# The first FFN product of batches 2 to 8 by Strassen's method, with the second weights streamed from HBM

## The chip, the cores and the metric

One core of a Trainium2 chip runs the program. The metric is device time in microseconds, median of three runs. Engines are called as in the profile: PE (TensorE matmul), PEld (its weight load), DVE (VectorE), ACT (ScalarE), POOL (GpSimd), SP (SyncE, which issues the DMAs here).

## What is computed

A local and global attention over 8 batches, 8 heads, 512 local and 32 global positions, head size 64, then a feed-forward network over all 8 x (512 + 32) tokens:

```python
x = attn_out.transpose(0, 2, 1, 3).reshape(B * S, H * D)     # 4352 x 512
h = x @ w_in                                                 # w_in: 512 x 2048
g = np.maximum(h, 0.0) + alpha * np.minimum(h, 0.0)
return (g @ w_out).astype(np.float32)                        # w_out: 2048 x 512
```

A local query sees the 32 global keys and the keys at most 32 positions away; a global query sees all keys. The weights arrive as float64.

## The kernel before

**Two streams in one loop.** The feed-forward work is cut into nine groups G: the eight batches' local tokens (512 columns each) and, last, all 256 global tokens. A group has 16 units, one per 128 of the 2048 hidden features (f). Unit t = 16 G + f does the first product `f1(t)` and, two units late (`LAG`), the second product `f2(t - 2)`. Attention goes on beside it: a head pair P (two heads of a batch, so four pairs per batch) is done in four steps u = 4 P + s, one per unit, with u = t + 19 (`NPRE`), so that a batch's attention is ready before its group begins. `attn(u, where)` is called at three places of a unit: "pre" before `f1`, "mid" after it, "post" between the two parts of `f2`. Head pairs 0 to 3 and most of pair 4 are done ahead of unit 0 in `prelude()`.

**Products in three terms.** Weights and activations are float32 and are split into a high part (a cast to float32r) and a low part (the rest); a product is high x high + low x high + high x low, three matmuls. `f1` contracts 512 = 4 x 128 channels, so 12 matmuls of 512 columns into one bank `h`, of which there are two. DVE turns `h` into `g` in two operations (L350, L351), ACT casts `gh` (L353), POOL forms `gl` (L354). `f2` part 0 multiplies `gh` by the two weight parts (8 matmuls), part 1 multiplies `gl` by the high part (4 matmuls), into four banks `o0` to `o3` that collect over the group's 16 units.

**Weights.** 32 pieces (f, j), j = 0 for w_in and 1 for w_out, are loaded as float64, decoded (`decode_words`, ACT, DVE and POOL) and split (`split_weights`) during the prelude and the first 12 or so units, and then stay in 32 of the 33 tiles of the pool `w`.

**Attention of a head pair.** Step 0: scores (`local_scores`, 64 small matmuls into two banks `s`) and softmax of both heads (DVE adds the mask and takes the minimum, ACT does eight exps); step 1: the sums' reciprocals and POOL's multiplication (`tail`); step 2: `values(P)`, which multiplies the values of the pair before (`pv_all`, into banks `s`), scores the global queries of this pair and writes `x_raw` (`pv_out`, ACT L319, L320), and then the global softmax. The probabilities must be transposed: for P below 8 (`NRAW`) by PE (`transpose_pe`, into banks `s`, copied to `pt`), later by DVE's 32x32 transposes (L287) and a round trip through HBM (`transpose_q`, `fetch_pt`). `split_x` splits `x_raw` into `xh` and `xl`, four channel blocks per group, in the last unit of the group before.

**What sets the order.** Matmuls stay in program order. For the other engines and SP a planner with a simulated time line picks, among the instructions that are ready, the one of highest priority; priority is program order, and attention's instructions are put ahead by 50. An engine executes its queue strictly in the order picked. All matmuls are recorded under the helper's line L88, so the tile names tell them apart: `h_ps`, `o`, `s_ps`, `o_ps`, `g_ps`, `pt`.

Of the kernel before, what the change touches and what calls it, by code (L numbers as in the profile page):

```python
# [8 lines left out]
F32 = mybir.dt.float32  # L9
F32R = mybir.dt.float32r  # L10
# [4 lines left out]
ALU = mybir.AluOpType  # L15
AX = mybir.AxisListType

NB, NH, SL, SG, D = 8, 8, 512, 32, 64
NPAIR = 4
DM, DF = 512, 2048  # L20
NF = DF // 128
NC = DM // 128
# [3 lines left out]
NEG = -8.0e9  # L26
WARM = (16, 12, 8, 8, 8)
NRAW = 8
NWB = 33
NST = 18  # L30
CLAMP_LO = 2.0**-15
CLAMP_HI = 122880.0 - 2.0**-7
TC = dict(schedule_with_timeline_sim=True)
HP = 50
NPRE = 19
HP0 = 400
LAG = 2
GOFF = 1024
GROWS = {1: (0, 0), 4: (0, 1), 7: (0, 2), 10: (1, 0), 13: (1, 1), 15: (1, 2)}
PRE = 3  # L40
RATE = (2, 1)
GROUPS = [("l", b) for b in range(NB)] + [("g", 0)]


# [12 lines left out]
def longformer_ffn(ctx: ExitStack, tc: tile.TileContext, qk, v, w, alpha, out):  # L57
    nc = tc.nc
# [3 lines left out]
    work = ctx.enter_context(tc.tile_pool(name="work", bufs=1))  # L62
    psum = ctx.enter_context(tc.tile_pool(name="psum", bufs=1, space=PS))

    dram = ctx.enter_context(tc.tile_pool(name="dram", bufs=1, space=bass.MemoryType.DRAM))
# [21 lines left out]
    def matmul(*a, **k):  # L87
        ins = nc.tensor.matmul(*a, **k)  # L88
        tc.keep_in_program_order(ins)
        return ins  # L90

    def stage(name, dtype=F32):
        return work.tile([128, 512], dtype, tag="st", name=name, bufs=NST)

    wraw, wts = {}, {}

    ordered = [True]

# [24 lines left out]

    def split_weights(f, j):
        t = wmid.pop((f, j))
        wt = wpool.tile([128, 2, 512], F32R, tag="w", name="wt")
        nc.scalar.copy(wt[:, 0, :], t)  # L127
        nc.gpsimd.tensor_tensor(wt[:, 1, :], t, wt[:, 0, :].bitcast(F32), op=ALU.subtract)  # L128
        wts[f, j] = wt

    consts = stage("consts")
    ident = consts[:, 384:512]
# [37 lines left out]
    def local_scores(P, warm=0):  # L170
        t = qks[P]
        sbanks[P] = [bank("h" if P < NPAIR and P % 2 else "s", "s_ps") for h in range(2)]
        keep_warm(sbanks[P][0], warm)
        masked = P < NRAW
        if masked:
            for h in range(2):
                matmul(sbanks[P][h], identb, bits, start=True, stop=False, skip_group_check=True)
        for i in range(4):
            for c in range(4):
                b = 4 * i + c  # L180
                k0 = NQ + 32 * start(b)
                for h in range(2):
                    th = t[64 * h : 64 * h + 64]
                    matmul(sbanks[P][h][32 * c : 32 * c + 32, 128 * i : 128 * i + 128], th[:, 32 * b : 32 * b + 32], th[:, k0 : k0 + 128], start=not masked, stop=True, skip_group_check=masked)
        ps[P] = work.tile([128, 1024], F32, tag="p", name="p", bufs=2)

    def p_tile(P, h, i):
        if P < NRAW:
# [78 lines left out]

    def new_pt(P):
        if P not in pts:
            pts[P] = work.tile([128, 1408], F32, tag="pt", name="pt", bufs=2)  # L270
        return pts[P]

    def transpose_pe(P, x, warm=0):
        pb = bank(f"o{x}" if P < NPAIR else "s", "pt")
        keep_warm(pb, warm)
        src, n = (ps[P][:, 512 * x : 512 * x + 512], 4) if x < 2 else (sg_sb, 3)
        for i in range(n):
            tc.keep_in_program_order(nc.tensor.transpose(pb[:, 128 * i : 128 * i + 128], src[:, 128 * i : 128 * i + 128], ident))  # L278
        copy("ada"[x], new_pt(P)[:, 512 * x : 512 * x + 128 * n], pb[:, 0 : 128 * n])
# [47 lines left out]
    def split_x(G, c):  # L327
        kind, b = GROUPS[G]
        n = SL if kind == "l" else NB * SG
        src = (x_raw if kind == "l" else x_glb)[:, c, 0:n]  # L330
        xh, xl = stage("xh", F32R), stage("xl", F32R)
        nc.scalar.copy(xh[:, 0:n], src)
        nc.vector.tensor_tensor(xl[:, 0:n], src, xh[:, 0:n].bitcast(F32), op=ALU.subtract)  # L333
        xs[G, c] = (xh, xl)

    gs, obs, gpart = {}, {}, {}

    def f1(T):
        G, f = divmod(T, NF)
        n = SL if GROUPS[G][0] == "l" else NB * SG  # L340
        h = bank("h", "h_ps")
        k = 0
        for c in range(NC):
            cs = slice(128 * c, 128 * c + 128)
            xh, xl = xs[G, c]
            for j, xt in ((0, xh), (1, xh), (0, xl)):
                matmul(h[:, 0:n], wts[f, 0][:, j, cs], xt[:, 0:n], start=(k == 0), stop=(k == 11))
                k += 1
        g = stage("g")
        nc.vector.tensor_scalar(g[:, 0:n], h[:, 0:n], 0.0, alpha_sb[:, f : f + 1], op0=ALU.min, op1=ALU.mult)  # L350
        nc.vector.scalar_tensor_tensor(g[:, 0:n], h[:, 0:n], 0.0, g[:, 0:n], op0=ALU.max, op1=ALU.add)  # L351
        gh, gl = stage("gh", F32R), stage("gl", F32R)
        nc.scalar.copy(gh[:, 0:n], g[:, 0:n])  # L353
        nc.gpsimd.tensor_tensor(gl[:, 0:n], g[:, 0:n], gh[:, 0:n].bitcast(F32), op=ALU.subtract)  # L354
        gs[T] = (gh, gl)

    def f2(T, part):
        G, f = divmod(T, NF)
        kind, b = GROUPS[G]
        n = SL if kind == "l" else NB * SG  # L360
        if f == 0 and part == 0:
            obs[G] = [psum.tile([128, 512], F32, tag=f"o{m}", name=f"o{m}", bufs=1) for m in range(NC)]
        o = obs[G]
        gh, gl = gs[T]
        for m in range(NC):
            ms = slice(128 * m, 128 * m + 128)
            if part == 0:
                matmul(o[m][:, 0:n], wts[f, 1][:, 0, ms], gh[:, 0:n], start=(f == 0), stop=False)
                matmul(o[m][:, 0:n], wts[f, 1][:, 1, ms], gh[:, 0:n], start=False, stop=False)
            else:  # L370
                matmul(o[m][:, 0:n], wts[f, 1][:, 0, ms], gl[:, 0:n], start=False, stop=(f == NF - 1))
        if part == 0:
            return
        del gs[T]
        if f == NF - 1:
            col = b * SL if kind == "l" else NB * SL
            for m in range(NC):
                st = stage("ost")
                copy("ad"[m % 2] if kind == "g" else "a", st[:, 0:n], o[m][:, 0:n])
                nc.sync.dma_start(out[m, :, col : col + n], st[:, 0:n])  # L380
# [52 lines left out]
    def attn(u, where):  # L433
        P, s = divmod(u, 4)
        if u == NPRE:
            if where == "mid":
                transpose_pe(P, 0)
                transpose_pe(P, 1)
            if where == "post":
                transpose_pe(P, 2)  # L440
                load_qk(P + 2)
            return
        if not (live(P) or live(P - 1)):
            return
        if (s, where) == (0, "pre") and live(P):
            local_scores(P)
        if s < 2 and where == "pre" and live(P):
            tails.append(softmax(P, s))
        if where == "mid":
            while tails:  # L450
                tails.pop()()
        if live(P) and P < NRAW:
            if (s, where) == (2, "pre"):
                transpose_pe(P, 0)
                transpose_pe(P, 1)
            if (s, where) == (3, "mid"):
                transpose_pe(P, 2)
        if (s, where) == (2, "mid"):
            gpart[P] = global_bank(P)
            values(P, "s")  # L460
            if live(P):
                load_v(P)
        if not live(P):
            return
        if (s, where) == (2, "post"):
            global_softmax(P)
            if live(P + 2):
                load_qk(P + 2)
        if P >= NRAW:
            if (s, where) == (2, "pre"):  # L470
                transpose_q(P, 0)
            if (s, where) == (3, "pre"):
                fetch_pt(P, 0)
                transpose_q(P, 1)
            if (s, where) == (3, "post"):
                fetch_pt(P, 1)
        if P == NRAW - 1 and (s, where) == (3, "post"):
            nc.gpsimd.memset(sg_sb[:, 288:384], 0.0)
# [35 lines left out]
    prelude()  # L514
    ordered[0] = False
    NT = len(GROUPS) * NF
    for t in range(NT + LAG):
        u = t + NPRE
        with tc.high_priority(offset=HP):
            attn(u, "pre")  # L520
        G, f = divmod(t + 1, NF)
        last = t + 1 < NT and f == 0
        if t < NT:
            f1(t)
        if last:
            for c in range(NC - 1):
                split_x(G, c)
        with tc.high_priority(offset=HP):
            attn(u, "mid")
        if last:  # L530
            split_x(G, NC - 1)
        if t >= LAG:
            f2(t - LAG, 0)
        with tc.high_priority(offset=HP):
            attn(u, "post")
        if t >= LAG:
            f2(t - LAG, 1)
        weights_step(RATE[t % 2])


_OUT = (NC, 128, NB * (SL + SG))
# [51 lines left out]
```

## Time and profile before

| | us |
|---|---|
| runs | 994.74, 995.45, 997.18 |
| median | 995.45 |
| profiled execution | 996.93, of which the span is 994.9 |
| PE busy | 940.0 of the span |
| DVE, ACT, POOL busy | 468.0, 350.3, 332.5 |
| unit 0 begins | 83.5 |
| global group | about 940 to the end |

The page gives busy time per engine, and groups of instructions as "line engine operation, output<-inputs, shape, count | busy, mean ns | idle before, releaser". The stage view gives the same busy times per stretch of the span, with the granted PE clock (1.00 is full), the share of time in which the DMA engines are busy, and GB/s. The chain is the sequence of work that ended last, as "start, us, what xcount"; the timeline has "start, us, engine line operation ... xcount [idle before <-releaser]". A busy PE overlaps its matmuls, so a matmul's own row is longer than its distance to the next one.

### The profile page before, as it was taken

How to read it: one execution, taken by the hardware profiler on the slowest of the kernel's cores; microseconds unless marked ns; L12 is line 12 of the kernel's file. 1: busy time of each engine (PE TensorE's matmuls, PEld its weight loads, DVE VectorE, ACT ScalarE, POOL GpSimd, SP SyncE). 2: the span in 40 equal slices, each digit the busy share in tenths (PEclk: the TensorE clock that was granted, in tenths of full speed). 3: DMA queues.
4: the chain of work that ended last, by engine and by line, in shares of the span. 5: the costliest groups of instructions: out<-in, count | busy, mean ns of one | idle time of the engine just before them, and what ended most of it. 6: DMA issues, size and time to landing. Idle time of an engine off the chain costs nothing.

```text
span 994.9 us, 19937 instructions
## 1 busy us (share of the span) xinstructions
PE 940.0 (94%) x7900; PEld 757.4 (76%) x7900; DVE 468.0 (47%) x1259; ACT 350.3 (35%) x1079; POOL 332.5 (33%) x301
## 2 busy tenths in 40 slices
PE   6645988999999999999999999999999999999998
PEld 5534766778787777877777777788778778888798
DVE  3667777654444544454445444544444443322322
ACT  4665556433333322342334322332333221210121
POOL 4357767622222222222222222222222222222222
PEclk8776898999999999999999999999999999999999
DMA  9454132135333434343344544354334331100010
GB/s 352 183 195 186 70 128 114 72 118 174 121 108 105 150 127 128 114 167 118 119 130 129 171 129 129 121 172 127 122 105 146 114 99 59 43 0 1 1 44 22
DMA packets 54095, 117.18 MB, mean 118 GB/s; under 512 B 18417, under 2 KB 34289, under 8 KB 50161
## 3 DMA queue, kind: packets, MB, share of 16 engines
q1 hardware_dynamic: 54000, 115.90, 34.7%
q8 instruction: 62, 1.02, 0.4%
q14 instruction: 33, 0.26, 0.1%
HBM read 89.66 MB, written 26.21 MB: 116 GB/s over the span
## 4 chain that ended last, share of the span: by engine, by line
PE 84%; DVE 6%; ACT 4%; issue 3%; POOL 2%; DMA 1%; SPq 0%; DVEq 0%; POOLq 0%; ACTq 0%
PE o L88 37%; PE h_ps L88 36%; PE o_ps L88 5%; PE g_ps L88 3%; PE s_ps L88 3%; DVE wt L116 2%; ACT p L201 1%; DVE wt L119 1%; DVE wt L118 1%; POOL wt L121 1%; DMA wraw<-in_w_dram 1%; ACT wt L114 1%; POOL wt L128 1%; DVE g L350 0%; ACT wt L127 0%
## 5 line engine op out<-in xcount | busy, mean ns | idle before, releaser
L88 PE MATMUL h_ps<-xh,wt 128*128 128x512 f32 (+1 forms) x1152 | 348.8, 385 | 0.0
L354 POOL TENSOR_TENSOR gl<-g,gh 128x512 fp32r<-128x512 f32 (+1 forms) x144 | 177.4, 1232 | 468.0 <-ACT gh L353 366.1
L88 PE MATMUL o<-gh,wt 128*128 128x512 f32 (+1 forms) x1152 | 284.4, 389 | 0.0
L353 ACT CAST gh<-g 128x512 fp32r<-128x512 f32 (+1 forms) x144 | 85.9, 596 | 465.5 <-DVE g L351 344.3
L88 PEld LDWEIGHTS h_ps<-xh,wt 128*128 128x128 f32 x1152 | 209.7, 188 | 50.3 <-issue 5.8
L88 PEld LDWEIGHTS o<-gh,wt 128*128 128x128 f32 x1152 | 208.3, 190 | 47.6 <-issue 0.2
L350 DVE TENSOR_SCALAR g<-h_ps,alpha_sb 128x512 f32<-128x512 f32 (+1 forms) x144 | 103.4, 718 | 279.6 <-PE h_ps L88 276.2
L88 PE MATMUL h_ps<-xl,wt 128*128 128x512 f32 (+1 forms) x576 | 220.3, 382 | 0.9 <-DVE xl L333 0.9
L88 PE MATMUL o<-gl,wt 128*128 128x512 f32 (+1 forms) x576 | 151.2, 384 | 0.0
L88 PEld LDWEIGHTS h_ps<-xl,wt 128*128 128x128 f32 x576 | 108.1, 188 | 24.5 <-DVE xl L333 1.1
L88 PEld LDWEIGHTS o<-gl,wt 128*128 128x128 f32 x576 | 105.4, 189 | 23.8
L217 POOL TENSOR_TENSOR p<-p,rz 128x512 f32<-128x512 f32 x64 | 65.8, 1046 | 124.0 <-DVE rz L212 124.0
L351 DVE SCALAR_TENSOR_TENSOR g<-h_ps,g 128x512 f32<-128x512 f32 (+1 forms) x144 | 95.2, 661 | 4.8
L207 ACT ACTIVATE p<-p,mn 128x128 f32<-128x128 f32 x192 | 74.4, 389 | 47.9 <-DVE mn L203 47.9
L203 DVE CUSTOM_DVE_ANT_0 p<-s_ps,mask 128x128 f32<-128x128 f32 x192 | 42.5, 287 | 57.1 <-PE s_ps L88 57.1
L88 PEld LDWEIGHTS o_ps<-pt,v 128*64 128x64 f32 x1536 | 53.2, 151 | 18.8 <-issue 9.1
L88 PE MATMUL o_ps<-pt,v 128*64 128x32 f32 (+1 forms) x1536 | 56.9, 235 | 6.9 <-ACT pt L264 4.7
L121 POOL TENSOR_TENSOR wt<-wt,wr 128x512 int32<-128x512 int32 x32 | 42.3, 1324 | 42.6 <-DVE wt L119 29.5
L287 DVE STREAM_TRANSPOSE p<-p 128x512 f32<-128x512 f32 x48 | 31.3, 690 | 50.1 <-POOL p L217 50.1
L128 POOL TENSOR_TENSOR wt<-wt 128x512 fp32r<-128x512 f32 x32 | 44.0, 1381 | 21.0 <-ACT wt L127 21.0
L88 PEld LDWEIGHTS s_ps<-qk 64*32 64x32 f32 x2048 | 29.9, 109 | 15.9 <-issue 14.2
L278 PE MATMUL pt<-consts,sg_sb 128*128 128x128 f32 x24 | 6.5, 400 | 35.4 <-ACT sg_sb L260 35.4
(66 smaller groups left out, 666.3 us busy)
## 6 DMA issues: line engine op xcount, KB each, us to landing
v<-in_v_dram SPq DMA_DIRECT2D x30, 1024.0 KB, 4.9
qk<-in_qk_dram SPq DMA_DIRECT2D x32, 672.0 KB, 6.1
wraw<-in_w_dram SPq DMA_DIRECT2D x32, 512.0 KB, 8.4
scratch<-p SPq DMA_DIRECT2D x96, 128.0 KB, 2.4
pt<-scratch SPq DMA_DIRECT2D x24, 512.0 KB, 3.4
out_dram<-ost SPq DMA_DIRECT2D x32, 256.0 KB, 2.3
scratch<-sg_sb SPq DMA_DIRECT2D x96, 48.0 KB, 1.9
pt<-scratch SPq DMA_DIRECT2D x24, 192.0 KB, 2.4
```

Of the source, the lines that this page charges most:

```text
L88: ins = nc.tensor.matmul(*a, **k)
L116: nc.vector.tensor_scalar(t, t, CLAMP_LO, CLAMP_HI, op0=ALU.max, op1=ALU.min)
L121: nc.gpsimd.tensor_tensor(ti, ti, r, op=ALU.add)
L128: nc.gpsimd.tensor_tensor(wt[:, 1, :], t, wt[:, 0, :].bitcast(F32), op=ALU.subtract)
L203: nc.vector.tensor_tensor_reduce(out=pr, in0=s[:, 128 * i : 128 * i + 128], in1=mask[:, i, :], scale=-0.125, scalar=3.0e38, op0=ALU.add, o ...
L207: nc.scalar.activation(pr, pr, AF.Exp, bias=mn[:, i : i + 1], scale=-1.0, accum_out=z[:, i : i + 1])
L217: nc.gpsimd.tensor_tensor(pr, pr, sc, op=ALU.mult)
L287: nc.vector.transpose(seg, seg)
L350: nc.vector.tensor_scalar(g[:, 0:n], h[:, 0:n], 0.0, alpha_sb[:, f : f + 1], op0=ALU.min, op1=ALU.mult)
L351: nc.vector.scalar_tensor_tensor(g[:, 0:n], h[:, 0:n], 0.0, g[:, 0:n], op0=ALU.max, op1=ALU.add)
L353: nc.scalar.copy(gh[:, 0:n], g[:, 0:n])
L354: nc.gpsimd.tensor_tensor(gl[:, 0:n], g[:, 0:n], gh[:, 0:n].bitcast(F32), op=ALU.subtract)
```

## The change

For groups 1 to 7 (units 16 to 127) two neighbouring units form a pair q. The hidden features (2 x 128), the channels (2 x 256) and the tokens (2 x 256) each have two halves, and the seven block products of Strassen's method (Winograd's form) replace the eight. Sums of weight blocks are formed once (`weight_sums`, units 12 to 26, from decoded weights that are stored in HBM and read back), and kept in place of w_out, whose split pieces go to HBM (`store_weights`) and are read back for each unit (`load_out_weights`, 512 KB, four tiles beside 28 fixed ones). Sums of token blocks are formed per batch, in place in `x_raw` (`x_sums`, in the last three units of the group before; all in unit 15 for group 1).

The even unit does four products of 256 columns, 24 matmuls, into the halves of both `h` banks; then ACT copies a half of `h0` and DVE makes three additions. The odd unit adds three products, 18 matmuls; DVE makes two more additions, and both halves' activations (`prelu`) follow, so that the even unit's `g` comes a unit later. The attention runs up to three units earlier (`CATCH`: two steps in units 16, 23 and 30). PE's transposes of P = 5 to 7 move from step 2 "pre" and step 3 "mid" to step 3 "pre", "mid" and "post". The `st` pool goes from 18 to 25 tiles, `w` from 33 to 32, `pt` and `p` from two to one (odd P below 8 take `p` from `w`).

```diff
+FAST = range(NF, NB * NF)
+CATCH = (16, 23, 30)
...
+    def product(dst, w, x, start):
+        for c in range(2):
+            for j, e in ((0, 0), (1, 0), (0, 1)):
+                matmul(dst, w[:, j, 128 * c : 128 * c + 128], x[e][:, 256 * c : 256 * c + 256], start=start, ...)
+                start = False
+
+    def f1_fast(T):
...
+        if f % 2 == 0:
+            hbs[G, q] = h0, h1 = bank("h", "h_ps"), bank("h", "h_ps")
+            product(h0[:, lo], we[:, :, lo], x("b11"), True)
+            product(h0[:, hi], wo[:, :, lo], x("t1"), False)
+            product(h1[:, hi], s24[q][:, :, lo], x("t2"), True)
+            product(h1[:, lo], s3[q // 2][:, :, o3 : o3 + 256], x("t3"), False)
+            u = us[G, q] = stage("u")
+            nc.scalar.copy(u[:, lo], h0[:, lo])
+            nc.vector.tensor_tensor(u[:, lo], u[:, lo], h1[:, hi], op=ALU.add)
+            nc.vector.tensor_tensor(u[:, hi], u[:, lo], h1[:, lo], op=ALU.add)
+            nc.vector.tensor_tensor(h1[:, hi], u[:, hi], h0[:, hi], op=ALU.add)
+            return
...
+        product(h0[:, hi], s24[q][:, :, hi], x("b22"), False)
+        product(h0[:, lo], we[:, :, hi], x("b21"), False)
+        product(h1[:, lo], wo[:, :, hi], x("t4"), False)
+        nc.vector.tensor_tensor(h0[:, hi], u[:, lo], h0[:, hi], op=ALU.add)
+        prelu(T - 1, h0, SL)
+        nc.vector.tensor_tensor(h1[:, lo], u[:, lo], h1[:, lo], op=ALU.add)
+        prelu(T, h1, SL)
...
+    def x_sums(G, step):
+        b11, b12, b21, b22 = x_part(0, 0), x_part(0, 1), x_part(1, 0), x_part(1, 1)
+        sub = lambda o, a, b: nc.vector.tensor_tensor(o, a, b, op=ALU.subtract)
+        if step == 0:
+            split_part(G, "b11", b11, False)
+            sub(b11, b12, b11)
+            split_part(G, "t1", b11, False)
+        if step == 1:
+            sub(b12, b22, b12)
+            sub(b11, b22, b11)
+            split_part(G, "t2", b11, False)
+            split_part(G, "t3", b12, True)
+        if step == 2:
+            split_part(G, "b22", b22, True)
+            split_part(G, "b21", b21, True)
+            sub(b21, b21, b11)
+            split_part(G, "t4", b21, True)
...
         if live(P) and P < NRAW:
-            if (s, where) == (2, "pre"):
+            if (s, where) == (3, "pre"):
                 transpose_pe(P, 0)
+            if (s, where) == (3, "mid"):
                 transpose_pe(P, 1)
-            if (s, where) == (3, "mid"):
+            if (s, where) == (3, "post"):
                 transpose_pe(P, 2)
...
+        if 2 <= t < NF + 2:
+            store_weights(t - 2)
+        if 10 <= t < 26 and t % 2 == 0:
+            load_sums((t - 10) // 2)
+        if 12 <= t < 28 and t % 2 == 0:
+            weight_sums((t - 12) // 2)
+        if NF <= t + 1 < NT:
+            load_out_weights(t + 1)
```

`weight_sums(q)` is four DVE additions of 256 columns, three ACT casts and three POOL subtractions (512, 256 and 256 columns); in `split_part` the last argument puts the subtraction on POOL instead of DVE. The global group keeps the old `f1`; the blocks of w_in that sums have overwritten are read back for it (`load_a21`).

More of the change, by code (lines that the diff above doesn't have):

```diff
@@ L28 @@
 NRAW = 8
-NWB = 33
-NST = 18
+NWB = 32
+NST = 25
 CLAMP_LO = 2.0**-15
@@ L93, in stage @@
         return work.tile([128, 512], dtype, tag="st", name=name, bufs=NST)
-    wraw, wts = {}, {}
+    wraw, wts, wos, a21 = {}, {}, {}, {}
+    wf = [dram.tile([128, 1024], F32, tag=f"wf{q}", name="wf") for q in range(NF // 2)]
+    wod = [dram.tile([128, 2, 512], F32, tag=f"wo{f}", name="wo") for f in range(NF)]
+    a21d = [dram.tile([128, 2, 2, 256], F32, tag=f"wa{q}", name="wa") for q in range(NF // 4)]
     ordered = [True]
@@ L125, in split_weights @@
         t = wmid.pop((f, j))
+        if j == 0:
+            nc.sync.dma_start(wf[f // 2][:, 512 * (f % 2) : 512 * (f % 2) + 512], t)
         wt = wpool.tile([128, 2, 512], F32R, tag="w", name="wt")
@@ L129, in split_weights, with store_weights, load_out_weights, load_a21 @@
         wts[f, j] = wt
+    def store_weights(f):
+        nc.sync.dma_start(wod[f], wts[f, 1].bitcast(F32))
+        if f % 2:
+            nc.sync.dma_start(a21d[f // 4][:, f // 2 % 2], wts[f, 0][:, :, 0:256].bitcast(F32))
+    def load_out_weights(T):
+        wos[T] = wpool.tile([128, 2, 512], F32R, tag="w", name="wo")
+        nc.sync.dma_start(wos[T].bitcast(F32), wod[T % NF])
+    def load_a21(q):
+        a21[q] = wpool.tile([128, 2, 2, 256], F32R, tag="w", name="a21")
+        nc.sync.dma_start(a21[q].bitcast(F32), a21d[q])
+    sums, s24, s3 = {}, {}, {}
+    def load_sums(q):
+        sums[q] = wpool.tile([128, 1024], F32, tag="w", name="wsum")
+        nc.sync.dma_start(sums[q], wf[q])
+    def weight_sums(q):
+        t = sums.pop(q)
+        a11, a12, a2a, a22 = (t[:, 256 * i : 256 * i + 256] for i in range(4))
+        nc.vector.tensor_tensor(a22, a2a, a22, op=ALU.add)
+        nc.vector.tensor_tensor(a2a, a11, a2a, op=ALU.subtract)
+        nc.vector.tensor_tensor(a11, a22, a11, op=ALU.subtract)
+        nc.vector.tensor_tensor(a12, a12, a11, op=ALU.subtract)
+        s24[q] = wpool.tile([128, 2, 512], F32R, tag="w", name="s24")
+        if q % 2 == 0:
+            s3[q // 2] = wpool.tile([128, 2, 512], F32R, tag="w", name="s3")
+        o3 = 256 * (q % 2)
+        for src, d in ((t[:, 0:512], s24[q]), (a22, wts[2 * q + 1, 0][:, :, 0:256]), (a2a, s3[q // 2][:, :, o3 : o3 + 256])):
+            nc.scalar.copy(d[:, 0, :], src)
+            nc.gpsimd.tensor_tensor(d[:, 1, :], src, d[:, 0, :].bitcast(F32), op=ALU.subtract)
     consts = stage("consts")
@@ L184, in local_scores @@
                     matmul(sbanks[P][h][32 * c : 32 * c + 32, 128 * i : 128 * i + 128], th[:, 32 * b : 32 * b + 32], th[:, k0 : k0 + 128], start=not masked, stop=True, skip_group_check=masked)
-        ps[P] = work.tile([128, 1024], F32, tag="p", name="p", bufs=2)
+        if P < NRAW and P % 2:
+            ps[P] = wpool.tile([128, 1024], F32, tag="w", name="p")
+        else:
+            ps[P] = work.tile([128, 1024], F32, tag="p", name="p", bufs=1)
     def p_tile(P, h, i):
@@ L269, in new_pt @@
         if P not in pts:
-            pts[P] = work.tile([128, 1408], F32, tag="pt", name="pt", bufs=2)
+            pts[P] = work.tile([128, 1408], F32, tag="pt", name="pt", bufs=1)
         return pts[P]
@@ L334, in split_x, with x_part, split_part @@
         xs[G, c] = (xh, xl)
+    def x_part(kh, th):
+        return x_raw[:, 2 * kh : 2 * kh + 2, 256 * th : 256 * th + 256]
+    def split_part(G, name, src, pool):
+        xh, xl = stage("xh", F32R), stage("xl", F32R)
+        vh, vl = (t.rearrange("p (c n) -> p c n", c=2) for t in (xh, xl))
+        nc.scalar.copy(vh, src)
+        (nc.gpsimd if pool else nc.vector).tensor_tensor(vl, src, vh.bitcast(F32), op=ALU.subtract)
+        xs[G, name] = (xh, xl)
+    def x_sums(G, step):
[15 more added lines that the diff above has]
+            split_part(G, "t4", b21, True)
     gs, obs, gpart = {}, {}, {}
@@ L345, in f1, with prelu @@
             xh, xl = xs[G, c]
+            w = wts[f, 0]
+            if GROUPS[G][0] == "g" and f % 2 and c < 2:
+                w = a21[f // 4][:, f // 2 % 2]
             for j, xt in ((0, xh), (1, xh), (0, xl)):
-                matmul(h[:, 0:n], wts[f, 0][:, j, cs], xt[:, 0:n], start=(k == 0), stop=(k == 11))
+                matmul(h[:, 0:n], w[:, j, cs], xt[:, 0:n], start=(k == 0), stop=(k == 11))
                 k += 1
+        prelu(T, h, n)
+    hbs = {}
+    def product(dst, w, x, start):
+        for c in range(2):
+            for j, e in ((0, 0), (1, 0), (0, 1)):
+                matmul(dst, w[:, j, 128 * c : 128 * c + 128], x[e][:, 256 * c : 256 * c + 256], start=start, stop=not start, skip_group_check=True)
+                start = False
+    def f1_fast(T):
+        G, f = divmod(T, NF)
+        q = f // 2
+        x = lambda name: xs[G, name]
+        we, wo = wts[2 * q, 0], wts[2 * q + 1, 0]
+        lo, hi = slice(0, 256), slice(256, 512)
+        o3 = 256 * (q % 2)
+        if f % 2 == 0:
[10 more added lines that the diff above has]
+            return
+        h0, h1 = hbs.pop((G, q))
+        u = us.pop((G, q))
+        product(h0[:, hi], s24[q][:, :, hi], x("b22"), False)
[5 more added lines that the diff above has]
+        prelu(T, h1, SL)
+    us = {}
+    def prelu(T, h, n):
+        f = T % NF
         g = stage("g")
@@ L364, in f2 @@
         gh, gl = gs[T]
+        w = wts[f, 1] if G == 0 else wos[T]
         for m in range(NC):
@@ L367, in f2 @@
             if part == 0:
-                matmul(o[m][:, 0:n], wts[f, 1][:, 0, ms], gh[:, 0:n], start=(f == 0), stop=False)
-                matmul(o[m][:, 0:n], wts[f, 1][:, 1, ms], gh[:, 0:n], start=False, stop=False)
+                matmul(o[m][:, 0:n], w[:, 0, ms], gh[:, 0:n], start=(f == 0), stop=False)
+                matmul(o[m][:, 0:n], w[:, 1, ms], gh[:, 0:n], start=False, stop=False)
             else:
-                matmul(o[m][:, 0:n], wts[f, 1][:, 0, ms], gl[:, 0:n], start=False, stop=(f == NF - 1))
+                matmul(o[m][:, 0:n], w[:, 0, ms], gl[:, 0:n], start=False, stop=(f == NF - 1))
         if part == 0:
@@ L374, in f2 @@
         del gs[T]
+        wos.pop(T, None)
         if f == NF - 1:
@@ L516, in longformer_ffn, with attention @@
     NT = len(GROUPS) * NF
+    steps = [[] for t in range(NT + LAG)]
+    u = NPRE
     for t in range(NT + LAG):
-        u = t + NPRE
+        steps[t] = [u, u + 1] if t in CATCH else [u]
+        u = steps[t][-1] + 1
+    def attention(t, at):
         with tc.high_priority(offset=HP):
[L520 to L523, printed above, removed]
+            if len(steps[t]) == 1:
+                attn(steps[t][0], at)
+                return
+            order = [(k, a) for k in range(2) for a in ("pre", "mid", "post")]
+            i = 2 * ("pre", "mid", "post").index(at)
+            for k, a in order[i : i + 2]:
+                attn(steps[t][k], a)
+    for t in range(NT + LAG):
+        attention(t, "pre")
+        if t in FAST:
+            f1_fast(t)
+        elif t < NT:
             f1(t)
+        G, f = divmod(t, NF)
+        last = G == NB - 1 and f == NF - 1
         if last:
             for c in range(NC - 1):
-                split_x(G, c)
-        with tc.high_priority(offset=HP):
-            attn(u, "mid")
+                split_x(G + 1, c)
+        attention(t, "mid")
         if last:
-            split_x(G, NC - 1)
+            split_x(G + 1, NC - 1)
+        if G < NB - 1:
+            for k, at in enumerate((15, 15, 15) if G == 0 else (13, 14, 15)):
+                if f == at:
+                    x_sums(G + 1, k)
         if t >= LAG:
             f2(t - LAG, 0)
-        with tc.high_priority(offset=HP):
-            attn(u, "post")
+        attention(t, "post")
         if t >= LAG:
@@ L538, in longformer_ffn @@
         weights_step(RATE[t % 2])
+        if 2 <= t < NF + 2:
[6 more added lines that the diff above has]
+            load_out_weights(t + 1)
+        if 122 <= t < 126:
+            load_a21(t - 122)
 _OUT = (NC, 128, NB * (SL + SG))
```

## The prediction

> **What bounds the kernel now.** I read the page's busy shares first, then the stages, then the chain of waits, then who made PE wait.
>
> ```profile
> PE 940.0 (94%) x7900; PEld 757.4 (76%) x7900; DVE 468.0 (47%) x1259; ACT 350.3 (35%) x1079; POOL 332.5 (33%) x301
> ...
> core 0: us, PE busy (x) PEld busy (x) DVE busy (x) ACT busy (x) POOL busy (x), PEclk, DMA share, GB/s
> 84.00:184.00 100.00, 83.99 (x686) 65.80 (x685) 76.97 (x126) 58.54 (x150) 69.44 (x55) 0.88 0.28 106
> 184.00:284.00 100.00, 98.15 (x843) 78.01 (x840) 47.69 (x154) 37.66 (x121) 32.53 (x29) 0.98 0.38 125
> 284.00:784.00 500.00, 500.00 (x4368) 399.63 (x4367) 230.57 (x742) 166.94 (x553) 135.09 (x114) 1.00 0.42 133
> 784.00:930.00 146.00, 146.00 (x857) 117.37 (x857) 47.03 (x95) 26.51 (x62) 35.44 (x29) 1.00 0.14 42
> 940.00:990.00 50.00, 50.00 (x401) 48.90 (x402) 15.41 (x35) 8.56 (x20) 11.82 (x16) 1.00 0.06 22
> ```
>
> From 284 us to 930 us PE has no idle time at all and a granted clock of 1.00; the other engines are under half busy. What counts there is the time of a matmul, and that is read from the chain, since a single matmul's row overlaps the next one:
>
> ```profile
> 849.99 1.87 PE h_ps L88 x8
> 851.85 2.80 PE o L88 x12
> ...
> 502.68 1.52 PE o_ps L88 x48
> 504.20 0.94 PE g_ps L88 x20
> ...
> 487.42 1.09 PE s_ps L88 x64
> ...
> 951.21 1.41 PE h_ps L88 x12
> 952.62 1.41 PE o L88 x12
> ...
> L88 PEld LDWEIGHTS h_ps<-xh,wt 128*128 128x128 f32 x1152 | 209.7, 188 | 50.3 <-issue 5.8 <-ACT xh L332 0.3
> ```
>
> Twelve matmuls of 512 columns take 2.80 us, 0.2334 us each. In the global batch, whose tiles are 256 columns wide, twelve take 1.41 us (951.21 to 952.62), 0.1177 us each. Both carry a 128x128 weight load per matmul, of 188 ns: it is hidden, and time goes by columns, with 0.001 us extra per matmul at half the width.
>
> **The first product, batches 2 to 8.** A pair of units (f even, f odd) now costs 24 x 0.2334 = 5.60 us of PE in the first product. After, it is 7 products x 2 halves of the contraction x 3 split terms = 42 matmuls of 256 columns, 42 x 0.1177 = 4.94 us. That is 0.66 us less per pair; 8 pairs x 7 batches = 56 pairs, **-36.8 us**. The second product keeps its 12 x 0.2334 = 2.80 us per unit; its weights merely come from another tile.
>
> If loads were not hidden, the 18 more per pair would cost 18 x 0.188 x 56 = 190 us. The global batch speaks against that: 0.1177 us from matmul to matmul is less than one load's 0.188. [...]
>
> **What the sums add on the other engines.**
>
> ```profile
> L350 DVE TENSOR_SCALAR g<-h_ps,alpha_sb 128x512 f32<-128x512 f32 x128 | 95.7, 748 | 248.0 <-PE h_ps L88 244.6 <-DMA scratch<-sg_sb 3.4
> L351 DVE SCALAR_TENSOR_TENSOR g<-h_ps,g 128x512 f32<-128x512 f32 x128 | 88.4, 691 | 4.3
> L350 DVE TENSOR_SCALAR g<-h_ps,alpha_sb 128x256 f32<-128x256 f32 x16 | 7.7, 484 | 31.6 <-PE h_ps L88 31.6
> L351 DVE SCALAR_TENSOR_TENSOR g<-h_ps,g 128x256 f32<-128x256 f32 x16 | 6.8, 424 | 0.6
> L264 ACT COPY ost<-o 128x256 f32<-128x256 f32 x2 | 0.6, 376 | 2.4 <-PE o L88 2.4
> L333 DVE TENSOR_TENSOR xl<-x_raw,xh 128x512 fp32r<-128x512 f32 x32 | 23.9, 766 | 2.6 <-ACT xh L332 2.3
> L332 ACT CAST xh<-x_raw 128x512 fp32r<-128x512 f32 x32 | 18.5, 626 | 0.1
> L319 ACT COPY x_raw<-o_ps 128x384 f32<-128x384 f32 x32 | 15.1, 473 | 10.5 <-PE o_ps L88 10.5
> L320 ACT COPY x_raw<-g_ps 128x128 f32<-128x128 f32 x32 | 8.5, 267 | 5.6 <-PE g_ps L88 5.6
> L354 POOL TENSOR_TENSOR gl<-g,gh 128x512 fp32r<-128x512 f32 x128 | 165.6, 1294 | 430.4 <-ACT gh L353 335.2 <-issue 54.7 <-PE g_ps L88 25.8
> L287 DVE STREAM_TRANSPOSE p<-p 128x512 f32<-128x512 f32 x48 | 31.3, 690 | 50.1 <-POOL p L217 50.1
> ```
>
> Per pair there are five DVE additions of 256 columns (no row has two of these operands and a PSUM output; between 0.42 and 0.48 us by L351 and L350, I take 0.45) = 2.25 us, and one ACT copy of 0.38 us. A unit with attention lasts 2.80 + 2.80 + (1.52 + 0.94 + 1.09)/4 = 6.49 us now and 6.16 us after. DVE: 230.57/500 x 6.49 = 2.99 us per unit, + 1.13, + 0.14 for the input sums (7 operations of 0.766 us per batch where 4 stand) = 4.26 us of 6.16, 69%. ACT: 2.17 + 0.19 + 0.12 (7 casts for 4) = 2.48 us, 40%. POOL: 1.75 + 0.32 (four splits per batch at 1.29) = 2.07 us, 34%. All fit, so these cost time only by their order.
>
> **The order around the two h banks.** One pair now holds both. Count from the end E of an odd unit's first product; DVE starts about 0.2 us after the matmuls it needs. The addition into h0 can start at E-0.5 (its two products end 6 matmuls before E), then 0.45 + 1.44 (0.75 + 0.69) free h0 at E+1.4, and the same again frees h1 at E+3.3. PE does the second product until E+2.8 and writes h1 only after 12 matmuls into h0, at E+4.2: 0.9 us of slack without attention. [...] Between even and odd units, the three additions end 0.2 + 3 x 0.45 = 1.6 us after E', and PE needs h0 at E'+2.8: 1.2 us of slack. So batch 8, which has no attention beside it, should run without a wait.
>
> With attention, this is the narrowest place:
>
> ```profile
> 488.88 0.40 ACT L207 ACTIVATE p<-p,mn 128x128 f32<-128x128 f32 x1 [2.03 <-DVE mn L203]
> ...
> 491.59 0.39 ACT L207 ACTIVATE p<-p,mn 128x128 f32<-128x128 f32 x1
> ```
>
> Both softmaxes' eight exps, at high priority, occupy ACT from 488.88 to 492.0, 3.1 us, starting 0.4 us after the scores. The copy of h0 queues behind them: scores end at E+3.9, exps at E+7.4, copy at E+7.8, three additions at E+9.2 (softmax's two short reciprocals lie before them); PE wants h0 at E+3.9+2.8+2.8 = E+9.5. Slack 0.3 us, once per head pair. Bounds over 23 head pairs: 0 to 1.3 us (DVE's 2 x 0.69 transposes in front as well), 0 to 30 us; near the lower end, since the transposes come after POOL's normalization; I take 0.15 each, **+3 us**.
>
> **Single places.** Batch 2's sums of x all fall on one unit, t = 15, behind the last head pair's output. Copy, subtraction twice, cast, subtraction: 0.2 + 0.7 (0.47 + 0.27) + 1.5 + 0.6 + 0.8 = 3.8 us after that output, and PE has 2.8 (second product) + 1.4 (two products into h0) = 4.2 us before it needs t2. Over the same units and up to t = 26, every second unit also forms sums of weights: DVE 4 x 0.42 = 1.7 us, which makes 8.5 + 1.7 = 10.2 of 12.3 us per pair, 83%. Nothing of this stands in the trace; 0 to 12 us (2 us in each of six pairs), I take **+4**. Input sums at the other six batches: 2.3 us of DVE in each of three units, of which PE's slack covers most; 0 to 2 us each, **+3** in all. If cover goes, PE stands at the first product of the next batch.
>
> **Transfers.**
>
> ```profile
> wraw<-in_w_dram SPq DMA_DIRECT2D x32, 512.0 KB, 8.4
> pt<-scratch SPq DMA_DIRECT2D x24, 512.0 KB, 3.4
> ```
>
> The second weights come at 512 KB per unit, 88 GB/s on top of 133: 221 GB/s. A load follows the end of unit t-1 and is used in unit t+2, two units and a first product later, 14 us, where a landing took 3.4 to 8.4 us. There are four tiles beside the 28 fixed ones, three are live, so SP doesn't stand behind a slot and the attention's loads and scratch writes behind it aren't held; they have three units of time anyway. The stores of split weights (early units) sit on SP too, 16 + 16 + 8 more issues: 0 to 3 us, I take 0: their sources are a step old. Giving up a second pt and p buffer costs nothing: each is free a unit before its next writer.
>
> **Transposes one unit later, batch 1.**
>
> ```profile
> PE pt L278 <- ACT sg_sb L260: 14.0, 4, 7.7
> PE o_ps L88 <- DVE pt L266: 2.2, 1, 2.2
> PE o_ps L88 <- ACT pt L264: 1.0, 1, 1.0
> ...
> 114.84 2.78 PE L88 MATMUL o_ps<-pt,v 128*64 128x32 f32 x48 [2.23 <-DVE pt L266]
> 119.41 3.02 PE L88 MATMUL o<-gh,wt 128*128 128x512 f32 x8
> ...
> 160.34 3.76 PE L88 MATMUL o<-gh,wt 128*128 128x512 f32 x8
> ...
> 170.22 2.03 PE L88 MATMUL o<-gh,wt 128*128 128x512 f32 x8
> ...
> 192.89 3.59 PE L88 MATMUL o<-gh,wt 128*128 128x512 f32 x8
> ```
>
> These are all of PE's waits from 84 to 300 us (without one of 0.7). The 7.7 us one belongs to P = 4 in unit t = 0, whose steps don't move. The other three on sg_sb (14.0 - 7.7 = 6.3) meet PE 1.9 us of second product and a transpose later, so all but about 0.5 goes; the waits of 2.2 and 1.0 are for banks that the transposes no longer hold then. 9 us of waits at most. After three of them, matmuls run slow: eight take 3.02, 3.76 and 3.59 us where 2.03 is usual, and 48 small ones 2.78 for 1.52, together 5.5 us. Bounds 0 and -14; two things are late next, the scores that follow the last transpose by only four matmuls, and ACT and DVE with decoding (77% DVE). I take **-10 us**.
>
> **Sum.** 996.93 (the profiled run; span 994.9 and 2.0 around it) - 36.8 - 10 + 3 + 4 + 3 = 960.1 us. The median of the runs is 995.45, 1.5 below, so I say **959 us**, 3.7% faster. Own range of this case 950 to 970.
>
> **Rivals.** (a) *All of it hidden*, every wait of batch 1 gone: 995.5 - 36.8 - 14 = 945 us. For it: PE has no wait from 284 to 930 us now. Against it: DVE goes from 46 to 69%. Chance 0.12. (b) *Half given back*: the ACT copy or the additions are late in the pairs beside attention, 0.45 us in 46 pairs, 21 us more: 980 us (970 to 991). For it: 0.3 us of slack. Chance 0.14. (c) *The other side: the pair's two h banks set the pace.* If DVE's order puts attention ahead of the additions, PE stands at each pair and its clock falls after it, as at 160 us. It decides from (36.8 + 10)/56 = 0.84 us per pair; at 1.3 us, the two transposes' price, it is 995.5 - 46.8 + 73 = 1022 us. For it: at 84 to 184 us, DVE 77% busy, PE 84%. Against it: those waits were for the global softmax, not h, and gaps of DVE before L350 (248 us over 128) are wide. Chance 0.08. (d) *No gain, within 0.3%* (3 us; about what this kernel's runs can tell from no change): stalls that just cancel, 0.04. (e) *Weight loads not hidden*: 959 + 190 = 1149 us by the trace's load, 0.01.
>
> **Chances.** Forecast 0.61, (a) 0.12, (b) 0.14, (c) 0.08, (d) 0.04, (e) 0.01: faster 0.87, same 0.04, slower 0.09. The range from 941 to 984 us takes in the forecast, nearly all of (a), and the nearer part of (b); it leaves out somewhat under 0.2.
>
> **What would show it.** First product of a pair 24 x 0.1177 = 2.82 and 18 x 0.1177 = 2.12 us in the chain; batch 8's unit 5.27 us instead of 5.60; no wait of PE on the five additions there. Beside attention, the wait to look for is PE's h_ps on DVE, at units with softmax. In batch 1 the waits on sg_sb shrink to one. The prediction is wrong if matmuls of 256 columns take over 0.135 us here, if PE waits on DVE in most pairs, or if PE waits for a weight transfer.

## The result, and the profile after

The changed kernel takes 1021.34 us in the median (1018.56 to 1022.39, four runs) where the kernel before takes 995.1: slower, ratio 1.0255, 95% interval 1.023 to 1.028. The profiled execution took 1022.39 us, its span is 1020.6.

First the page's busy line and the stage from 284 to 784 us, columns as before, which for the kernel before stood at PE 500.00, DVE 230.57 and a clock of 1.00:

```profile
PE 920.0 (90%) x8904; PEld 793.9 (78%) x8908; DVE 609.6 (60%) x1592; ACT 391.0 (38%) x1180; POOL 396.3 (39%) x353
...
284.00:784.00 500.00, 475.68 (x4995) 415.59 (x4993) 311.41 (x944) 186.50 (x605) 165.34 (x136) 0.98 0.63 209
```

PE has less to do, and has gaps. The chain in batch 8 shows that the product itself did what was said of it; 18 and 24 matmuls of 256 columns stand between two second products:

```profile
894.08 2.10 PE h_ps L90 x18
896.18 2.79 PE o L90 x12
898.97 2.80 PE h_ps L90 x24
901.77 2.80 PE o L90 x12
```

A pair's first product takes 2.10 + 2.80 = 4.90 us instead of 5.60; 0.70 x 56 = 39 us less. The step was predicted at 36.8. So 26 + 39 = 65 us were added elsewhere. Who makes PE wait, in all, from the view of waits (total us, times, longest us); `p` are the attention's probabilities, `x_glb L366` is DVE's copy of the global output out of its bank, `g L469` the second operation of an activation:

```profile
PE h_ps L90 <- DVE h_ps L451: 27.2, 16, 3.5
PE pt L322 <- POOL p L261: 24.1, 5, 10.1
PE pt L322 <- ACT sg_sb L304: 14.1, 2, 7.3
PE pt L322 <- DVE x_glb L366: 5.9, 3, 3.6
PE h_ps L90 <- DVE g L469: 4.8, 4, 2.8
PE h_ps L90 <- DVE xl L387: 4.6, 2, 2.5
```

In the kernel before, the waits for `p` were few:

```profile
PE pt L278 <- POOL p L217: 3.3, 2, 2.6
```

The first line of the longer list is the third addition of an even unit, and its 16 waits all lie after 300 us. They are not spread over the pairs: the timeline has them at units f = 14, 0 and 2 around a batch's end (3.5, 1.1 and 0.7 us in a typical one) and none in the middle of a batch, with attention or without. DVE's timeline at the end of batch 3 (unit 46) shows what comes before that addition, L451; L392 are the subtractions of token blocks, L387 their splits, L331 the attention's transposes:

```profile
440.44 1.15 DVE L387 TENSOR_TENSOR xl<-x_raw,xh 128x512 fp32r<-128x512 f32 x1 [0.30 <-ACT rz L255]
441.60 0.38 DVE L449 TENSOR_TENSOR u<-u,h_ps 128x256 f32<-128x256 f32 x1
441.90 1.44 DVE L392 TENSOR_TENSOR x_raw<-x_raw 128x512 f32<-128x512 f32 x1
443.26 0.41 DVE L450 TENSOR_TENSOR u<-u,h_ps 128x256 f32<-128x256 f32 x1
443.60 1.29 DVE L331 STREAM_TRANSPOSE p<-p 128x512 f32<-128x512 f32 x2
444.92 0.43 DVE L451 TENSOR_TENSOR h_ps<-u,h_ps 128x256 f32<-128x256 f32 x1
...
441.75 1.04 POOL L261 TENSOR_TENSOR p<-p,rz 128x512 f32<-128x512 f32 x1 [0.71 <-DVE rz L256]
...
445.49 0.76 PE L90 MATMUL h_ps<-xh,s 128*128 128x256 f32 x2 [3.53 <-DVE h_ps L451]
...
445.49 3.85 PE h_ps L90 x18
```

The three additions, 1.2 us of work, are strung out over 3.7 us; a subtraction takes 1.44 us while POOL multiplies beside it; PE waits 3.5 us, and then 18 matmuls take 3.85 us instead of 2.10: the granted clock is 0.57 from 445.49 to 449.34 us. Four of the six boundaries have such a wait, each with a subtraction of 1.43 to 1.44 us before it. Behind three of them the clock falls to 0.50 to 0.57; at 552.9 us it stays at 1.00, and the 18 matmuls are through in 2.2 us. The first and the last boundary have smaller waits (at most 1.8 and 2.3 us each, 3.9 and 3.5 us in all).

Ahead of 300 us the loss has two other places. Counted by the first matmul of a unit's second product, unit 2 begins at 112.0 us instead of 106.0, after longer waits of the prelude for `p`. And unit 15 to 16, where batch 2's sums of tokens meet the sums of weights, takes 19.0 us where 5.7 stood:

```profile
223.61 0.43 DVE L160 TENSOR_TENSOR wsum<-wsum 128x256 f32<-128x256 f32 x1 [2.30 <-DMA wsum<-wf]
...
224.69 0.58 PE L90 MATMUL h_ps<-xl,wt 128*128 128x256 f32 x1 [2.54 <-DVE xl L387]
229.70 0.58 PE L90 MATMUL h_ps<-xl,wt 128*128 128x256 f32 x1 [2.08 <-DVE xl L387]
```

DVE stands 2.3 us for a transfer of weights (`wsum`), with the split that PE needs queued behind it.

### The profile page after: what moved, and what is told of

Read it like the earlier page. It is cut to its first block, busy times and chain, and to the rows that moved or that the text cites. A ratio compares the mean times of both kernels' runs of the same rounds, so it can differ in the third digit from the quotient of the medians.

```text
span 1020.6 us, 23028 instructions
## 1 busy us (share of the span) xinstructions
PE 920.0 (90%) x8904; PEld 793.9 (78%) x8908; DVE 609.6 (60%) x1592; ACT 391.0 (38%) x1180; POOL 396.3 (39%) x353
## 4 chain that ended last, share of the span: by engine, by line
PE 54%; DVE 12%; ACT 8%; issue 4%; POOL 3%; DMA 2%; SPq 0%; DVEq 0%; ACTq 0%; POOLq 0%
PE o L90 24%; PE h_ps L90 23%; ACT p L251 4%; PE o_ps L90 3%; PE g_ps L90 2%; DMA wsum<-wf 2%; PE s_ps L90 2%; POOL xl L387 1%; DVE g L468 1%; DVE x_raw L392 1%; DVE g L469 1%; ACT ost L308 1%; POOL p L261 1%; DVE h_ps L451 1%; DVE u L449 1%
## 5 line engine op out<-in xcount | busy, mean ns | idle before, releaser
L90 PE MATMUL o<-gh,wo 128*128 128x512 f32 (+1 forms) x1024 | 248.9, 385 | 0.0
L90 PE MATMUL h_ps<-xh,wt 128*128 128x256 f32 (+1 forms) x1120 | 232.1, 303 | 6.4 <-DVE g L469 3.8
L90 PEld LDWEIGHTS o<-gh,wo 128*128 128x128 f32 x1024 | 177.8, 190 | 33.6 <-issue 0.4
L90 PE MATMUL h_ps<-xl,wt 128*128 128x256 f32 (+1 forms) x560 | 168.4, 301 | 5.4 <-DVE xl L387 4.6
L90 PE MATMUL h_ps<-xh,s 128*128 128x256 f32 x672 | 127.7, 287 | 30.7 <-DVE h_ps L451 27.2
L90 PEld LDWEIGHTS h_ps<-xh,s 128*128 128x128 f32 x672 | 107.3, 192 | 42.1 <-ACT xh L386 18.3
L90 PE MATMUL o<-gl,wo 128*128 128x512 f32 (+1 forms) x512 | 132.7, 381 | 0.0
L90 PEld LDWEIGHTS o<-gl,wo 128*128 128x128 f32 x512 | 92.6, 188 | 20.6
L469 DVE SCALAR_TENSOR_TENSOR g<-h_ps,g 128x512 f32<-128x512 f32 (+1 forms) x144 | 94.8, 659 | 3.1
L90 PE MATMUL h_ps<-xl,s 128*128 128x256 f32 x336 | 95.4, 284 | 0.0
L90 PEld LDWEIGHTS h_ps<-xl,s 128*128 128x128 f32 x336 | 64.5, 192 | 0.5 <-POOL xl L387 0.3
```

## The experiments

Two theories for the boundaries: *order* (the sums stand ahead of the pair's additions in DVE's queue; the same work in other places would be hidden) and *amount* (DVE, ACT and POOL have too much to do there). "Against the changed kernel" is the difference of two distances, each to the kernel before on the same chip; the changed kernel's distance is 26.2 us.

**Priority.** Around the pair's copy, additions and activations:

```diff
+            with tc.high_priority(offset=300):
                 nc.scalar.copy(u[:, lo], h0[:, lo])
...
```

> Only the order changes: the pair's copy, five additions and activations are put 300 instructions ahead in priority, so that the planner prefers them to token sums, transposes and softmax. Order theory (the waits of 3.5, 1.1 and 0.7 us at each batch boundary come from the order of DVE's queue): these waits go, the cold clock after them too, some 6 us at each of six boundaries, about 985 us, faster than before's 995. Amount theory (DVE, ACT and POOL have too much work in those three units): the wait moves to the next batch's first products (on xh, xl), and the time stays within 5 us of 1021.

1017.67 us, ratio 1.0236 (1.0217 to 1.0254); 3 us less than the changed kernel, with intervals that overlap, so no gain is shown. It doesn't tell the theories apart, because DVE's order at unit 46 stayed the same:

```profile
442.56 1.43 DVE L392 TENSOR_TENSOR x_raw<-x_raw 128x512 f32<-128x512 f32 x1
443.92 0.41 DVE L451 TENSOR_TENSOR u<-u,h_ps 128x256 f32<-128x256 f32 x1
444.25 1.29 DVE L331 STREAM_TRANSPOSE p<-p 128x512 f32<-128x512 f32 x2
445.57 0.43 DVE L452 TENSOR_TENSOR h_ps<-u,h_ps 128x256 f32<-128x256 f32 x1
```

A priority only chooses among instructions that the planner's time line has ready. That the sums are still picked first would follow if the additions become ready later there than on the chip; no run shows the planner's times, so this stays open.

**The sums left out.**

```diff
-                if f == at:
+                if f == at and G == 0:
                     x_sums(G + 1, k)
+                elif f == at and k == 2:
+                    for name in ("b11", "t1", "t2", "t3", "b22", "b21", "t4"):
+                        xs[G + 1, name] = xs[G, name]
```

> Groups 2 to 7 use the token sums and splits of group 1 again; the sums of batches 3 to 8 are left out (subtractions, casts and splits). Both theories have the boundaries free of waits: 1021 less about 40 us, 978 to 985 us. If the boundaries' loss is neither (transfers, or the attention's phase against the pairs), the waits on the third addition stay at units f = 14 and the time stays above 1005 us. The difference between this and the run with priorities is what the sums' own work costs when the order is right.

984.16 us, 0.989 (0.9871 to 0.991): 37 us against the changed kernel, and from 300 us on the 27.2 us of waits shrink to

```profile
PE h_ps L90 <- DVE h_ps L451: 1.1, 5, 0.2
```

So six boundaries cost 37 us, 6.2 each on average. PE's waits are some 28 of these (after 300 us 27.2 on the third addition and 1.5 on `g`, less this 1.1); the slow matmuls behind three waits are about 7, an estimate from the chain's rows against their usual lengths. The attention beside the pairs costs next to nothing, since it stands here as before.

**The subtractions left out**, the splits and casts kept:

```diff
-        sub = lambda o, a, b: nc.vector.tensor_tensor(o, a, b, op=ALU.subtract)
+        sub = lambda o, a, b: None if G > 1 else nc.vector.tensor_tensor(...)
```

> The changed kernel without the four 512-column subtractions per batch for batches 3 to 8 (left out; the seven splits and casts of what then stands in x_raw stay). Leaving everything out brought 37 us. If DVE's time is what counts, the subtractions are 2.8 of 5.1 us of DVE's work per boundary, so they bring a bit over half, 995 to 1003 us. If the chain counts (each split waits for a cast and that for a subtraction, with POOL and ACT in turn), they bring nearly all of it, 985 to 992 us.

986.79 us, 0.9918 (0.9904 to 0.9931): 34 of the 37 us. A little over half of DVE's work for the sums makes nearly all of the loss: it isn't DVE's time that adds up, but the chain of subtraction, cast and split, or simply a load that just passes the slack. With the subtractions go the four of 1.44 us beside POOL, and the time that DVE stands before the last one of each batch, which in the changed kernel is

```profile
DVE x_raw L392 <- POOL xl L387: 31.3, 7, 4.7
```

The run takes both away together.

**Order by hand.** Each step of the sums is issued on DVE and ACT behind the pair's last operation written before it:

```diff
+                    with tc.issue_after(pin["v"].ins), tc.issue_after(pin["a"].ins):
                         x_sums(G + 1, k)
```

> The priorities didn't change DVE's order at the boundaries (the third addition still came behind two 512-column subtractions and two transposes). Here the order is set by hand: for batches 3 to 8 each step of token sums is issued on DVE and ACT behind the pair's last operations that were written before it. Order theory: the 3.5 us wait at units f = 14 and the cold matmuls behind it go, some 5 us at five boundaries, 993 to 1001 us. Amount theory: the wait moves to the next batch's t2, t3 or t4, 1015 to 1025 us.

1012.78 us, 1.0171 (1.0151 to 1.0192), 9 us better. At unit 46 the wait shrinks to 0.7 us. But the next places grow:

```profile
441.12 0.43 DVE L451 TENSOR_TENSOR h_ps<-u,h_ps 128x256 f32<-128x256 f32 x1
441.46 1.28 DVE L392 TENSOR_TENSOR x_raw<-x_raw 128x512 f32<-128x512 f32 x2
442.67 1.30 DVE L331 STREAM_TRANSPOSE p<-p 128x512 f32<-128x512 f32 x2
443.89 0.40 DVE L458 TENSOR_TENSOR h_ps<-u,h_ps 128x256 f32<-128x256 f32 x1
444.20 1.75 DVE L387 TENSOR_TENSOR xl<-x_raw,xh 128x512 fp32r<-128x512 f32 x1
...
453.62 0.69 DVE L392 TENSOR_TENSOR x_raw<-x_raw 128x512 f32<-128x512 f32 x1 [4.57 <-POOL xl L387]
```

Now the split of t2, at 1.75 us beside POOL's, holds up the odd unit's activations (1.0 us of PE), and the last subtraction still has DVE stand 4.6 us for POOL's split of the block that it overwrites. PE's wait on the third addition at f = 0 (unit 48) is 1.7 us, where it was 1.1. Neither theory's number: order is part of it.

**Spread only.** The first step in unit 12 (b11's split, the first subtraction), the split of t1 in 13, the rest in 14 and 15:

```diff
-            for k, at in enumerate((15, 15, 15) if G == 0 else (13, 14, 15)):
+            for k, at in enumerate((15, 15, 15, 15) if G == 0 else (12, 13, 14, 15)):
```

> Only the spreading: the first step of the sums in unit 12, the split of t1 in 13, the rest in 14 and 15 as before; no order set by hand, and the last subtraction in place. Place theory (an earlier start is what helps): within 5 us of the run with the whole boundary part. Order theory (the planner will again put the sums ahead of the pair's additions wherever they are written): 1010 to 1020 us.

1003.1 us, 1.0073 (1.0049 to 1.0097): 19 us better, more than the order theory gave it and less than the place theory did. The waits of 3.5 us at f = 14 are gone; at f = 0 there is one of 1.7 to 2.3 us at each boundary.

**Spread, ordered, and the last subtraction written elsewhere** (`sub(b12, b21, b11)`, into a block that has been split already):

> The changed kernel with only the boundary part of the version that beat both: sums spread over units 12 to 15, their DVE and ACT work issued behind the pair's, the last subtraction writing to a free block. That version is 42 us below the changed kernel; the later start of the pairs and the buffers account for 12 and 6 on their own. If the boundaries are the rest: 24 us, 995 to 1000 us. If the parts don't add up (the boundary part brings nearly the 37 us of leaving the sums out): 984 to 990 us.

991.51 us, 0.9964 (0.9951 to 0.9977): 30 of the 37 us, with all the work done. From 300 us on, PE's waits for the third addition are, of this kernel and of the one only spread:

```profile
PE h_ps L90 <- DVE h_ps L452: 7.2, 5, 1.5
...
PE h_ps L90 <- DVE h_ps L452: 15.0, 12, 2.3
```

What is left in the first line are waits of 1.3 to 1.5 us at f = 2. Those at f = 0, 1.7 to 2.9 us with the order by hand and 1.7 to 2.3 us with the spreading, are gone, and DVE's 31.2 us of standing for POOL's split before the last subtraction (in both of those runs) are down to 1.2. In the run only spread, ACT does the pair's copy of `h0`, which the additions need, behind the cast of that subtraction's result (451.68 and 450.78 us at unit 48). So the place of the sums removes the waits at f = 14, and the free block fits the end of those at f = 0. But no run has the free block without the order by hand, so how the last 12 us divide between these two isn't shown.

This settles the boundaries: the same sums in other places, in another order and with another destination are nearly hidden. Amount alone falls.

**Batch 2's first step earlier.**

```diff
-            for k, at in enumerate((15, 15, 15) if G == 0 else (13, 14, 15)):
+            for k, at in enumerate((13, 15, 15) if G == 0 else (13, 14, 15)):
```

> The changed kernel with the first of batch 2's three steps of token sums in unit 13 instead of 15 (its input is ready since unit 7); the rest is unchanged. If the loss of unit 15 (19.0 us where 5.7 stood, five waits of 0.6 to 2.5 us on xh and xl of the first products) is the length of the chain of casts and subtractions: some 5 us less, 1014 to 1017 us. If it is the amount of work together with the sums of weights, 1019 to 1022 us.

1020.7 us, 1.0259 (1.0244 to 1.0275): no gain. Unit 15 to 16 became 20.5 us, with one wait of 7.5 us on a cast of x, and unit 17 to 18 shorter by 3.7: the loss only moved.

**Pairs from group 2 on**, weight sums in units 18 to 32:

```diff
-FAST = range(NF, NB * NF)
+FAST = range(2 * NF, NB * NF)
...
-        if 12 <= t < 28 and t % 2 == 0:
-            weight_sums((t - 12) // 2)
+        if 18 <= t < 34 and t % 2 == 0:
+            weight_sums((t - 18) // 2)
```

> Pairs begin with group 2 (batch 3); batch 2 has the old first product and the old splits, and the sums of weights are formed in its units (18 to 32) instead of 12 to 26. Eight pairs fewer save 8 x 0.69 = 5.5 us less. If the 16 us lost between unit 15 and 20 come from batch 2's token sums at unit 15 and from forming weight sums just ahead of their use, about 12 us net faster than the changed kernel, 1007 to 1012 us. If the loss only moves on to unit 31, 1021 to 1027 us.

1009.14 us, 1.0134 (1.0117 to 1.0152): 13 us better although eight pairs are given up, so the start at unit 15 cost some 13 + 5.6, about 18 us. Unit 15 to 16 takes 8.3 us here. The token sums and the weight sums leave this place together, so their shares aren't told apart.

**Two p buffers again:**

```diff
-        if P < NRAW and P % 2:
-            ps[P] = wpool.tile([128, 1024], F32, tag="w", name="p")
-        else:
-            ps[P] = work.tile([128, 1024], F32, tag="p", name="p", bufs=1)
+        ps[P] = work.tile([128, 1024], F32, tag="p", name="p", bufs=2)
```

> The probabilities of odd head pairs below 8 no longer take a tile of the weights' pool; p has two buffers again, and st 23 tiles instead of 25. In the changed kernel's prelude the second pair's softmax starts 10 us later than before and unit 2 comes 5.5 us later. If the buffers' place is what holds it: unit 2 about 5 us earlier, 1015 to 1017 us. If it is the planner's order for another reason (stores, more tiles), no change, 1019 to 1023 us; fewer st tiles may cost some at the boundaries.

1014.58 us, 1.0186 (1.0169 to 1.0203); 7 us better, and unit 2 begins at 106.2 us. The prelude's loss is the p tile in the weights' pool (or the two more st tiles, given up here as well; no run separates them).

**The transposes alone**, moved in the kernel before, with one pt buffer and two more st tiles:

> The kernel before, with only the transposes of P = 5 to 7 one step later, one pt buffer instead of two, and two more tiles in the pool st. My prediction's step: 7 to 10 us faster than before, 985 to 988 us. Rival, from the trace of the changed kernel (PE waits for DVE's copy of x_glb, 1.2, 1.2 and 3.6 us, ahead of the first transpose, whose bank that copy releases): waits on sg_sb are only replaced, 993 to 998 us.

990.97 us, 0.9961 (0.9947 to 0.9975), 4 us faster, between the two numbers. PE's waits, in the kernel before and, behind the dots, in this one:

```profile
PE pt L278 <- ACT sg_sb L260: 35.4, 7, 7.7
...
PE pt L278 <- ACT sg_sb L260: 31.0, 4, 8.1
PE pt L278 <- DVE x_glb L322: 6.9, 3, 2.9
```

Four waits on sg_sb instead of seven, so those of P = 5 to 7 are gone as predicted, but three for x_glb have come, since the first transpose needs the bank that this copy releases.

**A version that beats both**: from group 2 on with the weight sums in units 18 to 32, two p buffers (w with 31 tiles), and the boundary part.

> All that the single runs pointed to, together: pairs from group 2 on (-12), two p buffers (-6; the pool w has 31 tiles), the order of the boundary's operations set by hand (-8), and the token sums spread over four units (b11 and the first subtraction in unit 12, the split of t1 in 13) with the last subtraction writing to a block that POOL doesn't read just then. If these add up: 995 us or a little less, the same as before. If spreading frees the boundaries (the loss is where the sums stand, not how much they are): 975 to 985 us, faster than before by over 1%. If the amount is what counts: 995 to 1003 us.

979.36 us, 0.9833 (0.9817 to 0.9848): 1.7% faster than the kernel before, 42 us better than the changed kernel. That is more than the sum by single parts that I had expected, because spreading was still unmeasured then. Now that all three parts are measured singly they add up to 51 us (13, 7 and 30): together they bring less than apart.

**The weight sums ordered too**, in that version:

> The version that beat both, with the sums of weights too issued behind the pair's or unit's own operations. It lost about 9 us to the kernel before between units 16 and 36, where they stand. If they delay the units' own operations: 973 to 977 us. If the loss there has another cause (units with two steps of attention, a bank not yet free): 978 to 981 us.

976.36 us, 0.9814 (0.9796 to 0.9833). The intervals overlap, so no gain over the version without it is shown.

## Why the prediction was wrong

959 us was forecast, 3.7% faster; 1021 us was measured, 2.6% slower. Point by point:

- *First product, -36.8 us*: right; 0.70 us a pair, 39 us. 256 columns cost 0.1167 us a matmul (2.80/24), less than the 0.192 to 0.195 us that a weight load of this product takes on the mean, so the loads stay hidden.
- *Order around the h banks; beside attention +3*: right. The first addition into `h0` starts 1.60 us after the odd unit's first matmul (895.51 for 893.91 us by the timeline), when twelve are through, and in none of the 56 pairs earlier; so here it comes behind both products in its bank, at E-0.5 as forecast. Batch 8 runs at 4.9 and 5.6 us a unit from unit 114 on, and pairs beside attention have no wait in the middle of a batch: the run without sums leaves 1.1 us in all.
- *Input sums at the other batches, +3 us*: **the step that failed**; 37 us, 6.2 per boundary where 0.5 was taken and 2 was the upper bound. I had added 2.3 us of DVE per unit and set that against PE's slack, as if they stood where there is room. (By the kernel's steps it is three, three and one operation, so 2.3, 2.3 and 0.8 us: the amount was, if anything, taken too high.) Four things were missing. The order: the planner put them, and the transposes, between the additions. Their length beside POOL: the trace groups the subtractions as

```profile
L392 DVE TENSOR_TENSOR x_raw<-x_raw x28: 649/693/1436, 225.4 to 880.1; 128x512 f32<-128x512 f32 x28
```

  and the four at 1.43 to 1.44 us all overlap a POOL operation by 0.89 us. The standing queue: ahead of the last subtraction DVE stands for POOL's split, with all that is queued behind it (31.3 us in seven waits). And the clock after the wait (0.50 to 0.57 behind three of the four waits of 3.5 us), whose price I had read in batch 1 (eight matmuls in 3.76 us for 2.03) but not put into this term.
- *Batch 2's sums and the weights' sums, +4, at most 12*: about 18 us. The chain of 3.8 us was counted as if DVE were free; it shared DVE with weight sums that waited for their own transfer. I had looked for a weight transfer that PE waits for, not DVE.
- *Transposes, -10 us*: right that the sg_sb waits go; new waits on the bank (6.9 us) take the place of what went, and -4 is left; the granted clock of the profiled execution, over its whole span, rises from 0.964 to 0.973. I had named DVE's decoding as what is late next, but not priced it.
- *Giving up a p buffer, nothing*: wrong, 7 us in the prelude.
- *Transfers of w_out*: right; PE never waits for them. (512 KB in 6.16 us are 85 GB/s, not 88; the stage shows 209 GB/s in all, where 221 were forecast.)

Together: -39 + 37 + 18 + 7 - 4 = +19 of the 26 us measured; 7 us aren't placed, and by the timeline most of them lie between units 2 and 37. The terms are differences between single runs, and such differences need not add up. Rival (c), 1022 us, gave the time by luck, not by its mechanism: it had every pair wait for attention at 1.3 us. In fact 16 waits do it, and what is ahead of the additions is the change's own sums. Nearest to a warning was its evidence, DVE at 77% and PE at 84% in batch 1, which I set aside because those waits had another name.

## What to carry to other kernels

When a change puts new work on an engine with spare time, ask at which moment it stands in that engine's queue and what critical operation is behind it; a mean share (69% by the forecast, 62% in the stage from 284 us) says nothing of the six places where all of it falls. A short wait of the bounding engine can be paid more than once: behind three of the four waits of 3.5 us the granted clock was 0.50 to 0.57, and 18 matmuls took 3.85 to 4.18 us instead of 2.10. If work must be added at a boundary, spread it over the units before, let it be issued behind the critical operations, and keep it from overwriting what another engine still reads: the same work then cost 7 us instead of 37.

## What the runs showed of the hardware

DVE's subtractions of token blocks, with both inputs in SBUF, took longer where a POOL operation was already under way: of 28 subtractions 23 take 0.65 to 0.69 us, one that POOL overlaps by 0.21 us takes 0.76, and the four that began after POOL's operation and overlap it by 0.89 us take 1.43 to 1.44 us. In the other order POOL's operation was the longer one: four subtractions that began before POOL's multiplication and overlapped it by 0.57 us kept their 0.69, and the multiplication took 1.47 us there instead of 1.04. The pair's additions, with one input in PSUM, take at most 0.43 us, also the 43 that POOL overlaps by more than 0.2 us.

Behind three of the changed kernel's four waits of 3.5 us the granted clock is 0.50 to 0.57 over the next 18 matmuls (3.85 to 4.18 us for 2.10); behind the fourth, at 552.9 us, it stays 1.00. In the run with priorities 18 matmuls take 2.2 us behind the wait of 3.5 us at 446.15 us. After 300 us in the changed kernel, single waits of 0.5 to 1.8 us and one of 2.3 us are followed by a clock of 1.00, while two waits of 1.1 and 0.8 us close together, at 963 and 964 us, are followed by 0.50. So the length of one wait doesn't tell whether the clock falls; what does isn't shown here.
